# Second MLP in five sets of token tiles instead of four, and a first-MLP unit whose second token half begins a 512-byte line

## The chip, the cores and the metric

The kernel runs on one NeuronCore of a Trainium2 chip. Five engines work side by side, each with its own queue that it works off in order: TensorE (PE in the profile; its weight loads are shown apart as PEld), VectorE (DVE), ScalarE (ACT), GpSimd (POOL) and SyncE (SP, which here issues DMAs). The metric is the device time of one execution in microseconds (us), the median of several runs.

## The reference

Three blocks follow each other, all in float32 (the weights of both MLPs come as float64):

```
attn = softmax(mask(q k^T / 8)) v            # 4 batches, 8 heads, 576 tokens, head size 64
x    = attn as (4, 576, 512)

h    = relu(x @ w_in)                        # first MLP, 512 -> 1024
c    = conv over tokens, width 3, of h       # per channel
x    = (h * sigmoid(c)) @ w_out              # 1024 -> 512

u    = x + real(fft2(x))                     # over tokens and channels
un   = (u - mean) / sqrt(var + 1e-6)         # per token
out  = u + relu(un @ w_ch1) @ w_ch2          # second MLP, 512 -> 2048 -> 512
```

## The kernel before, in words

Matmuls run on float32 numbers rounded to fp32r. Each operand is split into a high and a low part, and a product takes three matmuls (`mm3`: high by high, high by low, low by high).

No instruction is issued where the code makes it. Every call records a piece of work with its reads, its writes, a due time (`key`) and a guessed duration for each engine that may do it. At the end `P.order()` (line 292) walks through a simulated time, gives each engine the ready piece of work with the earliest due time, and so fixes the order of every engine's queue and, where several engines may do a copy, the engine. A change of the recorded work thus also moves its neighbours.

**First MLP.** The work is cut into units: batch `b` (576 tokens) and slice `f` (128 of the 1024 channels), 32 in all. `m1` (line 644) computes a unit's hidden slice, the convolution and the gate, and writes the gated slice in its high part `gh` and low part `gl` into the tile `hid`. Both are stored with the second half of the tokens in reverse order, so that the Fourier transform can fold the halves. `m2` (line 672) uses 128-token pieces of `gh` and `gl` as the stationary operand of matmuls with 512 output columns, into banks 4 to 7 of PSUM. The pieces start at the columns in `COLS`; the 32 tokens left over of each half are copied into the tiles `g9`, which are multiplied once per two batches (`shared_tile`). 2304 tokens so make 18 tiles of 128: 16 regular ones and two shared ones, which stand at places 8 and 17 of the list `order`.

**Transform.** `dft(b, ...)` does the Fourier transform of a batch from small tables (tile `tb`) and writes u. For the batches 0 and 1 it also normalises the tiles (`ln`: statistics and a Newton square root on DVE, scaling on ACT, four transposes on PE, a split into high and low parts). Batch 0 goes straight into `first4`, batch 1 over DRAM (`to_dram`). The later tiles are normalised during the second MLP (`ln_set`).

**Second MLP.** The tiles are processed in sets (`SETS`, line 947). For a set and a slice `f` of 128 of the 2048 channels, `n1` (line 981) multiplies weights with the set's normalised tiles: up to 512 tokens are one matmul wide, a set of five tiles is done as two halves of 320. ACT makes the high part of the hidden slice, DVE the low part. `n2` (line 1003) multiplies 128-token pieces of it with the second weights, one PSUM bank per tile, over all `f`. `runs` (line 949) lists which set runs over which `f` with which banks; set 0 runs in two parts. The first eight slices' weights have homes in space that the first MLP leaves free; the last eight are converted from float64 (`W2.convert`, four DVE instructions and a copy each, through two buffers `raw`) while the second run is under way, since their space is the transform's.

`h_bank` hands out the PSUM banks 2 and 3 in turn for `n1`, so an `n1` can't begin before the low part of the one before the last has been read out of its bank by DVE.

Of the kernel before, what the change touches and what calls it, by code (L numbers as in the profile page):

```python
# [11 lines left out]
F32 = mybir.dt.float32  # L12
F32R = mybir.dt.float32r
# [9 lines left out]
B, H, S, D = 4, 8, 576, 64  # L23
DM, FF1, FF2 = 512, 1024, 2048
NF1, NF2 = FF1 // 128, FF2 // 128
HS = S // 2
# [165 lines left out]
class Plan:  # L192
# [79 lines left out]
    def mm3(self, o, ah, al, bh, bl, first, last):  # L272
        self.mm(o, ah, bh, first, False)
        self.mm(o, ah, bl, False, False)
        self.mm(o, al, bh, False, last)
# [142 lines left out]
def tile_kernel(ctx: ExitStack, tc: tile.TileContext, forms, qt_in, ktp, ktd, vtp, vtd, wm1, wm2, conv_w,  # L418
                tab, mask, ident16_in, ident_in, out):
    nc = tc.nc  # L420
    ctx.enter_context(tc.manual_schedule())
    P = Plan({"ACT": nc.scalar, "DVE": nc.vector, "POOL": nc.gpsimd, "PE": nc.tensor, "SP": nc.sync})
    mm, mm3, dma = P.mm, P.mm3, P.dma
# [11 lines left out]
    def copy(out_, in_, engines=("ACT",), key=None):  # L435
        n = out_.n()
        psum = in_.tile.pool is banks
        t = {"ACT": on_act(n), "DVE": on_dve(n, False, psum), "POOL": on_pool(n)}
        P.run({e: t[e] for e in engines}, "copy", key, out=out_, in_=in_)
# [4 lines left out]
    def lo_of(out_, src, hi, key=None):  # L444
        n, psum = out_.n(), src.tile.pool is banks
        dve("tensor_tensor", on_dve(n, True, psum), key, out=out_, in0=src, in1=hi.bitcast(F32), op=ALU.subtract)
# [11 lines left out]
    bank = [banks.tile([128, 512], F32, f"pb{i}", whole=True) for i in range(8)]  # L458
# [20 lines left out]
    win = stg.tile([128, 512], I32, "win")  # L479
    moe = pool_of("moe", reuse_waits="tile")  # L480
    x_odd = moe.tile([128, 4, 2, S], F32R, "x")
    hid_t = moe.tile([128, 2, 2, 640], F32R, "hid")
    cv_t = moe.tile([128, S], F32, "cv")
    g_t = moe.tile([128, S], F32, "g")
    hpad = [moe.tile([128, S + 2], F32, "hp") for _ in range(2)]
    moe.fill(-moe.size)
    gh_t, gl_t = ([hid_t[:, i, l, :S] for i in range(2)] for l in range(2))

    low = pool_of("low", reuse_waits="tile")
    g9h, g9l = (low.tile([128, NF1, 128], F32R, "g9") for _ in range(2))  # L490
# [147 lines left out]
        dve("tensor_tensor", 0.1, out=convw, in0=a, in1=r, op=ALU.add)  # L638


    COLS = [0, 128, 288, 416]
    hid = {}

    def m1(b, f, h_banks, at):
        s = NF1 * b + f
        w = W1.tiles[0, f]
        hp = hpad[s % 2]
        for half in range(2):
            o = of("h", h_banks)[:, :HS]
            sl = slice(HS * half, HS * half + HS)  # L650
            with P.products(at + 4.3 * half):
                for c in range(4):
                    wsl = slice(128 * c, 128 * c + 128)
                    mm3(o, w[:, 0, wsl], w[:, 1, wsl], xT[b][:, c, 0, sl], xT[b][:, c, 1, sl], c == 0, c == 3)
            P.run({"ACT": 0.41}, "activation", out=hp[:, 1 + HS * half:1 + HS * half + HS], in_=o, func=AF.Relu,
                  scale=0.5)
        cv, g = cv_t, g_t
        P.run({"ACT": 0.78}, "mul", out=cv, in_=hp[:, 1:S + 1], mul=convw[:, NF1 + f:NF1 + f + 1])
        dve("scalar_tensor_tensor", 0.81, out=cv, in0=hp[:, 0:S], scalar=convw[:, f:f + 1], in1=cv,
            op0=ALU.mult, op1=ALU.add)  # L660
        dve("scalar_tensor_tensor", 0.88, out=cv, in0=hp[:, 2:S + 2],
            scalar=convw[:, 2 * NF1 + f:2 * NF1 + f + 1], in1=cv, op0=ALU.mult, op1=ALU.add)
        P.run({"ACT": 0.69}, "activation", out=cv, in_=cv, func=AF.Tanh)
        dve("scalar_tensor_tensor", 0.54, out=g[:, 0:289], in0=cv[:, 0:289], scalar=1.0, in1=hp[:, 1:290],
            op0=ALU.add, op1=ALU.mult)
        dve("scalar_tensor_tensor", 0.48, out=g[:, 289:576], in0=cv[:, 575:288:-1], scalar=1.0,
            in1=hp[:, 576:289:-1], op0=ALU.add, op1=ALU.mult)
        gh, gl = hid[s] = gh_t[s % 2], gl_t[s % 2]
        copy(gh, g, ("ACT", "POOL"))
        lo_of(gl, g, gh)  # L670

    def m2(b, f, at):
        gh, gl = hid[NF1 * b + f]
        w = W1.tiles[1, f]
        for i in range(4):
            c0 = COLS[i]
            with P.products(at + 2.15 * i):
                mm3(bank[4 + i], gh[:, c0:c0 + 128], gl[:, c0:c0 + 128], w[:, 0], w[:, 1], f == 0, f == NF1 - 1)
        for src, dst in ((gh, g9h), (gl, g9l)):
            sv = src.bitcast(F32).rearrange("p (t s) -> p t s", t=2)[:, :, 256:288]  # L680
            dv = dst[:, f, :].rearrange("p (t s) -> p t s", t=2)[:, :, 32 * (b % 2):32 * (b % 2) + 32]
            P.run({"ACT": 0.235, "POOL": 0.45}, "copy", out=dv, in_=sv)

# [98 lines left out]
    def ln(us, puts, bank_of, at):  # L782


        n = len(us)
        mv = D_["mv"]()[:, :n]
        sq = D_["sq"]()
        v, r, t = (sq[:, i, :n] for i in range(3))
        for i in range(n):
            st = D_["st"]()  # L790
            dve("bn_stats", 0.68, out=st, in_=us[i])
            dve("bn_aggr", 0.17, out=mv[:, i], in_=st)
        small = lambda op_, **kw: dve(op_, 0.16, **kw)
        small("tensor_scalar", out=v, in0=mv[:, :, 1], scalar1=1e-6, scalar2=None, op0=ALU.add)

        small("tensor_scalar", out=r.bitcast(I32), in0=v.bitcast(I32), scalar1=-0.5,
              scalar2=float(0x5F3759DF), op0=ALU.mult, op1=ALU.add)
        small("tensor_scalar", out=v, in0=v, scalar1=-0.5, scalar2=None, op0=ALU.mult)
        for _ in range(3):
            small("tensor_tensor", out=t, in0=r, in1=r, op=ALU.mult)  # L800
            small("tensor_tensor", out=t, in0=t, in1=v, op=ALU.mult)
            small("scalar_tensor_tensor", out=r, in0=t, scalar=1.5, in1=r, op0=ALU.add, op1=ALU.mult)
        small("scalar_tensor_tensor", out=t, in0=mv[:, :, 0], scalar=-1.0, in1=r, op0=ALU.mult, op1=ALU.mult)
        for i in range(n):
            P.run({"ACT": 0.62}, "activation", out=us[i], in_=us[i], func=AF.Identity, scale=r[:, i:i + 1],
                  bias=t[:, i:i + 1])
            bt = bank_of()
            with P.products(at):
                for c in range(4):
                    P.turn(bt[:, 128 * c:128 * c + 128], us[i][:, 128 * c:128 * c + 128], ident)  # L810
            hi, lo, done = puts[i]()
            b4 = bt.rearrange("p (c n) -> p c n", c=4)
            copy(hi, b4)
            lo_of(lo, b4, hi)
            done()

    def to_dram(i):

        ns = D_["ns"]()
        return ns[:, 0], ns[:, 1], lambda: dma(n_dram[i], ns.rearrange("p l c n -> p l (c n)").bitcast(F32))  # L820
# [21 lines left out]
    def dft(b, at, every):  # L842
# [4 lines left out]
        when = [at - every]  # L847
# [52 lines left out]
        for m, T in enumerate((AT, BT)):  # L900
            for l in range(2):
                src = T[:, l, :, 256:288].bitcast(F32)
# [34 lines left out]
        if bp:  # L937
            y9 = yload(16 + pr)
            finish(16 + pr, y9, *products(lambda l, c: t9[0][:, l, c], lambda l, c: t9[1][:, l, c], a09))
            if b == 1:  # L940
                ln([y9], [lambda: to_dram(8)], df, when[0] + 8)
        pair(0)

    SETS = (range(0, 4), range(4, 9), range(9, 14), range(14, 18))
    R0 = 8
    runs = ((0, 0, R0, (4, 5, 6, 7)), (1, 0, 16, (0, 1, 4, 5, 6)), (0, R0, 16, (7, 0, 1, 4)),
            (2, 0, 16, (5, 6, 7, 0, 1)), (3, 0, 16, (4, 5, 6, 7)))  # L950
    hidden, rings, sets = {}, {}, []

    def un_load(p):
        for i, k in enumerate(SETS[p]):
            dma(sets[0][:, :, :, 128 * i:128 * i + 128].bitcast(F32),
# [100 lines left out]
    for k in range(2 * NF1):  # L1056
        _, i, f = W1.todo[k]
# [61 lines left out]
    for r, f in seq:  # L1119
        if r == 0:  # L1120
            begin[r, f] = T4 + 14 + 7.5 * f, 7.5
        else:
            step = 1.38 * len(SETS[runs[r][0]])
            begin[r, f] = at, step
            at += step
    lns = ({(2, 9 + i): (2, (i,)) for i in range(5)})
    lns.update({(3, 3 + i): (3, (i,)) for i in range(4)})
    for k, (r, f) in enumerate(seq):
        if (r, f) == (1, 0):
            later = pool_of("set", "left", (low,), reuse_waits="tile")  # L1130
            sets.append(later.tile([128, 2, 4, 640], F32R, "unt"))
            un_load(1)
        if (r, f) == (1, 2):
            wpb = pool_of("wpb", "right", (D_["pool"], keep), reuse_waits="tile")
            rest = [wpb.tile([128, 2, 512], F32R, "wf") for _ in range(2 * NF1)]
            ln_tiles_of(wpb)
            rings["u"].views += [wpb.tile([128, DM], F32, "uu") for _ in range(3)]
            rings["o"].views += [wpb.tile([128, DM], F32, "oo") for _ in range(2)]
            wpb.fill(TOP - wpb.size)
            for j in range(2 * NF1):  # L1140
                W2.convert(rest[j], raws[j % 2])
        at, step = begin[r, f]
        if (r, f) in lns:
            p, ids = lns[r, f]
            ln_set(p, ids, at + step * 0.9)
        n1(runs[r][0], f, at, step)
        n2(r, f, at + step, step)
# [80 lines left out]
```

## Time and profile before

| | us |
|---|---|
| runs | 775.37, 776.19, 777.86 (median 776.19) |
| profiled execution | 778.47 |
| its span, first to last instruction | 776.7 |
| PE busy | 744.8 (96%) |
| DVE busy | 486.7 (63%) |
| ACT busy | 308.6 (40%) |
| POOL busy | 135.9 (17%) |

The profiled execution is 2.28 us above the median of the runs; 1.8 us of it lie outside the span. PE is busy through nearly all of the span. Busy time alone says little where matmuls overlap: the distance from the start of one group of matmuls to the start of the next is what a group costs. The granted clock of TensorE is 1.00 where it runs at 2.4 GHz and 0.50 at 1.2 GHz.

The stretches of the span: attention of the first batch until about 60 us, attention beside the first MLP until about 250, first MLP beside the transforms until about 345, transforms beside the first part of set 0 until about 412, and the rest of the second MLP until 773.

### The profile page before, as it was taken

The numbers are of one execution on the slowest core, as the hardware profiler recorded it, in microseconds if no ns is written. First come the engines' busy times: TensorE is split into PE (matmuls) and PEld (weight loads), VectorE is DVE, ScalarE is ACT, GpSimd is POOL, SyncE is SP. The second block draws the span as 40 slices with busy tenths as digits, with TensorE's granted clock in tenths as the row PEclk, the third lists the DMA queues.
The fourth block names the chain that finished last, engine by engine and source line by source line (L and its number), as shares of the span: only waits on it lengthen the run. The fifth ranks groups of instructions, "written<-read, shape, count | busy, mean of one in ns | idle before, by whom it ended". The sixth has DMA issues, their size and how long they took to land.

```text
span 776.7 us, 11954 instructions
## 1 busy us (share of the span) xinstructions
PE 744.8 (96%) x4438; PEld 663.2 (85%) x4438; DVE 486.7 (63%) x1155; ACT 308.6 (40%) x792; POOL 135.9 (17%) x151
## 2 busy tenths in 40 slices
PE   5889989999999999989999999999999999999997
PEld 4779879998999998867788999988889999988886
DVE  5989989889888788979677667317544111121112
ACT  3877766675667655434332122112212111101110
POOL 4654424542445112201000000000000000000000
PEclk9979999999999999989999999999999999999999
DMA  9944354223412835357947333005131000030001
GB/s 239 254 152 134 107 164 139 88 72 111 152 48 90 285 120 163 107 190 250 330 162 246 136 133 135 1 1 163 42 105 32 28 1 1 1 122 1 1 0 55
DMA packets 38976, 88.58 MB, mean 114 GB/s; under 512 B 4351, under 2 KB 9859, under 8 KB 38790
## 3 DMA queue, kind: packets, MB, share of 16 engines
q1 hardware_dynamic: 38262, 84.66, 34.1%
q0 software_dynamic: 432, 2.97, 1.0%
q8 instruction: 35, 0.57, 0.3%
q10 hardware_dynamic: 224, 0.18, 0.1%
q14 instruction: 23, 0.19, 0.1%
HBM read 65.23 MB, written 22.44 MB: 113 GB/s over the span
## 4 chain that ended last, share of the span: by engine, by line
PE 53%; DVE 1%; ACT 0%; issue 0%; ACTq 0%
PE pb L259 53%; DVE y L246 0%; DVE hid L246 0%; DVE win L246 0%; DVE pm L246 0%; DVE raw L246 0%; DVE hp L246 0%; DVE pp L246 0%; ACT pq L246 0%; ACT pm L246 0%; ACTq L246 0%
## 5 line engine op out<-in xcount | busy, mean ns | idle before, releaser
L259 PE MATMUL pb<-wf,hid 128*128 128x512 f32 x1140 | 291.5, 397 | 1.2 <-DVE hid L246 1.2
L259 PEld LDWEIGHTS pb<-wf,hid 128*128 128x128 f32 x1140 | 207.6, 189 | 39.1 <-DVE hid L246 1.6
L246 DVE SCALAR_TENSOR_TENSOR hid<-pb,hid 128x320 fp32r<-128x320 f32 (+1 forms) x96 | 53.5, 557 | 186.5 <-ACT hid L246 186.4
L246 ACT ACTIVATE hid<-pb 128x320 fp32r<-128x320 f32 (+1 forms) x96 | 47.1, 491 | 256.7 <-PE pb L259 256.7
L259 PE MATMUL pb<-x,wf 128*128 128x288 f32 x768 | 116.6, 302 | 3.3 <-DVE wf L246 2.0
L259 PEld LDWEIGHTS pb<-x,wf 128*128 128x128 f32 x768 | 108.8, 191 | 7.0 <-DVE wf L246 2.2
L259 PE MATMUL pb<-unt,wf 128*128 128x320 f32 x672 | 103.6, 309 | 0.0
L259 PEld LDWEIGHTS pb<-unt,wf 128*128 128x128 f32 x672 | 100.8, 188 | 2.3
L246 POOL PARTITION_ALL_REDUCE mx<-sm x56 | 82.9, 1486 | 80.6 <-DVE sm L246 39.5
L259 PE MATMUL pb<-wf,wf 128*128 128x512 f32 x336 | 85.1, 400 | 3.6 <-DVE hid L246 3.6
L259 PEld LDWEIGHTS pb<-wf,wf 128*128 128x128 f32 x336 | 64.0, 193 | 17.5 <-DVE hid L246 4.3
L605 ACT ACTIVATE xb<-pb,rs 72x64 f32<-72x64 f32 (+1 forms) x224 | 51.2, 309 | 13.2 <-DVE rs L246 12.9
L246 DVE SCALAR_TENSOR_TENSOR cv<-hp,convw,cv 128x576 f32<-128x576 f32 x64 | 55.4, 866 | 1.3 <-ACT cv L246 0.7
L259 PEld LDWEIGHTS pb<-VT,sm 104*72 104x72 f32 (+1 forms) x448 | 41.0, 157 | 8.6 <-ACT sm L246 6.8
L259 PE MATMUL pb<-VT,sm 104*72 104x65 f32 (+1 forms) x448 | 42.8, 240 | 5.6 <-ACT sm L246 5.6
L259 PE MATMUL pb<-QT,KT 128*104 128x144 f32 (+1 forms) x224 | 44.3, 323 | 1.6 <-ACT sm L246 1.1
L259 PEld LDWEIGHTS pb<-QT,KT 128*104 128x104 f32 (+1 forms) x224 | 36.1, 191 | 7.5 <-issue 4.9
L246 ACT ACTIVATE hp<-pb 128x288 f32<-128x288 f32 x64 | 26.6, 416 | 29.9 <-PE pb L259 28.5
L246 DVE TENSOR_TENSOR wf<-raw,wf 128x512 fp32r<-128x512 f32 x44 | 31.7, 722 | 6.9 <-ACT wf L246 6.6
L246 DVE SCALAR_TENSOR_TENSOR raw<-raw,win 128x512 uint32<-128x512 uint32 x48 | 34.9, 727 | 0.9
L246 DVE SCALAR_TENSOR_TENSOR win<-raw,win 128x512 int32<-128x512 int32 x48 | 34.7, 723 | 1.0
L246 POOL CAST g<-hid 128x64 fp32r<-128x64 f32 x43 | 22.4, 528 | 73.4 <-ACT hid L246 37.1
(143 smaller groups left out, 842.6 us busy)
## 6 DMA issues: line engine op xcount, KB each, us to landing
raw<-in_wm_dram SPq DMA_DIRECT2D x48, 512.0 KB, 4.5
y<-yd SPq DMA_DIRECT2D x18, 256.0 KB, 4.2
ud<-y SPq DMA_DIRECT2D x18, 256.0 KB, 3.5
QT<-in_qt_dram SPq DMA_DIRECT2D x31, 144.0 KB, 3.4
fd<-fs SPq DMA_DIRECT2D x8, 514.0 KB, 3.9
fl<-fd SPq DMA_DIRECT2D x8, 514.0 KB, 6.3
yd<-y SPq DMA_DIRECT2D x16, 256.0 KB, 2.2
uu<-ud SPq DMA_DIRECT2D x16, 256.0 KB, 3.1
```

Source lines behind the costliest of these rows:

```text
L246: getattr(self.engines[eng], name)(**a)
L259: getattr(self.engines["PE"], name)(*[v.real() for v in a], **kw)
L605: nc.scalar.mul(out=x[:, i], in_=p[:, i], mul=r[:, i:i + 1])
```

## The change

- The sets become 4, 4, 4, 4 and 2 tiles instead of 4, 5, 5 and 4. All but the last then run `n1` as one 512-wide matmul per weight piece, the last as one 256-wide.
- The shared tile at place 8 now begins set 2 instead of ending set 1. Its normalisation inside `dft(1, ...)` goes; `ln_set` makes it later.
- The half-unit layout in `hid`: the second token half begins at column 384 (1536 bytes) instead of 288 (1152 bytes), and the pieces start at 0, 128, 384 and 512. The tile grows from 640 to 768 columns. The writes of `gh` and `gl` become two stretches of 288 instead of one of 576.
- `unt`, the tile of normalised tokens, shrinks from 640 to 512 columns; the scratch of GpSimd's DMAs from 2048 to 1024 bytes.

```diff
-    hid_t = moe.tile([128, 2, 2, 640], F32R, "hid")
+    hid_t = moe.tile([128, 2, 2, 768], F32R, "hid")
...
-    gh_t, gl_t = ([hid_t[:, i, l, :S] for i in range(2)] for l in range(2))
+    gh_t, gl_t = ([hid_t[:, i, l].rearrange("p (t s) -> p t s", t=2)[:, :, :HS] for i in range(2)] for l in range(2))
...
-    COLS = [0, 128, 288, 416]
+    COLS = [(0, 0), (0, 128), (1, 0), (1, 128)]
...
-        copy(gh, g, ("ACT", "POOL"))
-        lo_of(gl, g, gh)
+        gs = g.rearrange("p (t s) -> p t s", t=2)
+        copy(gh, gs, ("ACT", "POOL"))
+        lo_of(gl, gs, gh)
...
-                mm3(bank[4 + i], gh[:, c0:c0 + 128], gl[:, c0:c0 + 128], w[:, 0], w[:, 1], f == 0, f == NF1 - 1)
+                mm3(bank[4 + i], gh[:, t, c0:c0 + 128], gl[:, t, c0:c0 + 128], w[:, 0], w[:, 1], f == 0, f == NF1 - 1)
...
-            if b == 1:
-                ln([y9], [lambda: to_dram(8)], df, when[0] + 8)
...
-    SETS = (range(0, 4), range(4, 9), range(9, 14), range(14, 18))
+    SETS = (range(0, 4), range(4, 8), range(8, 12), range(12, 16), range(16, 18))
     R0 = 8
-    runs = ((0, 0, R0, (4, 5, 6, 7)), (1, 0, 16, (0, 1, 4, 5, 6)), (0, R0, 16, (7, 0, 1, 4)),
-            (2, 0, 16, (5, 6, 7, 0, 1)), (3, 0, 16, (4, 5, 6, 7)))
+    runs = ((0, 0, R0, (4, 5, 6, 7)), (1, 0, 16, (0, 1, 4, 5)), (0, R0, 16, (6, 7, 0, 1)),
+            (2, 0, 16, (4, 5, 6, 7)), (3, 0, 16, (0, 1, 4, 5)), (4, 0, 16, (6, 7)))
...
-    lns = ({(2, 9 + i): (2, (i,)) for i in range(5)})
+    lns = {(2, 9 + i): (2, (i,)) for i in range(4)}
     lns.update({(3, 3 + i): (3, (i,)) for i in range(4)})
+    lns.update({(4, 5 + i): (4, (i,)) for i in range(2)})
...
-            sets.append(later.tile([128, 2, 4, 640], F32R, "unt"))
+            sets.append(later.tile([128, 2, 4, 512], F32R, "unt"))
...
-    nc = _bacc.Bacc("TRN2", target_bir_lowering=False, num_devices=1, dynamic_dma_scratch_size=2048)
+    nc = _bacc.Bacc("TRN2", target_bir_lowering=False, num_devices=1, dynamic_dma_scratch_size=1024)
```

What stands in the queues, first on PE in the second run (`pb_128` and `pb_129` are the PSUM banks 2 and 3, `pb_126`, `127`, `130`, `131`, `132` the banks 0, 1, 4, 5 and 6; `unt` the set's tokens, `hid` the hidden slice). Before, one slice `f` is:

```order
L259 MATMUL pb_129<-unt,wf 128x320 x12
L259 MATMUL pb_128<-unt,wf 128x320 x12
L259 MATMUL pb_126<-wf,hid 128x512 x3
L259 MATMUL pb_127<-wf,hid 128x512 x3
L259 MATMUL pb_130<-wf,hid 128x512 x3
L259 MATMUL pb_131<-wf,hid 128x512 x3
L259 MATMUL pb_132<-wf,hid 128x512 x3
```

After, two slices of the second run are:

```order
L259 MATMUL pb_129<-unt,wf 128x512 x12
L259 MATMUL pb_126<-wf,hid 128x512 x3
L259 MATMUL pb_127<-wf,hid 128x512 x3
L259 MATMUL pb_130<-wf,hid 128x512 x3
L259 MATMUL pb_131<-wf,hid 128x512 x3
L259 MATMUL pb_128<-unt,wf 128x512 x12
```

Per slice there are 39 matmuls before and 24 after, for five tiles and for four. The last run of the changed kernel has, per slice, twelve matmuls of 256 columns and six of 512.

The second place is on DVE, at the end of the first MLP. `hid<-pb_129` reads the result of set 0's first `n1` out of bank 3; `y` are tiles of u, `st`, `mv` and `sq` the statistics of `ln`. Before:

```order
L246 TENSOR_TENSOR pp<-pq,pm 128x258
L246 TENSOR_TENSOR pm<-pq,pm 128x258
L246 TENSOR_TENSOR y<-y,pp 128x255
L246 TENSOR_TENSOR y<-y,pm 128x257
L246 BN_STATS st<-y 128x6
L246 BN_AGGR mv<-st 128x2
...
L246 SCALAR_TENSOR_TENSOR sq<-mv,sq 128x1
L246 SCALAR_TENSOR_TENSOR g<-cv,hp 128x287
L246 SCALAR_TENSOR_TENSOR hid<-pb_129,hid 128x512
```

After:

```order
L246 TENSOR_TENSOR hid<-g,hid 128x2x288
L246 SCALAR_TENSOR_TENSOR hid<-pb_129,hid 128x512
L246 SCALAR_TENSOR_TENSOR win<-raw,win 128x512
L246 SCALAR_TENSOR_TENSOR raw<-raw,win 128x512
L246 COPY y<-pb_130 128x512
L246 TENSOR_TENSOR pp<-pq,pm 128x258
L246 TENSOR_TENSOR pm<-pq,pm 128x258
L246 TENSOR_TENSOR y<-y,pm 128x257
L246 TENSOR_TENSOR y<-y,pp 128x255
```

The shared tile's statistics are gone from here, and the read of bank 3 has moved ahead of the four instructions that finish that tile. Further on in the same queue, the changed kernel has the copy of the second shared tile out of bank 2 (`o<-pb_128`), which ACT did before, behind the statistics of batch 1's first two tiles:

```order
L246 SCALAR_TENSOR_TENSOR sq<-mv,sq 128x2
L246 TENSOR_TENSOR o<-y 128x255 x2
L246 TENSOR_TENSOR fo<-fo,o 128x255 x2
L246 TENSOR_TENSOR fo<-y 128x2
L246 COPY o<-pb_128 128x512
L246 TENSOR_TENSOR e_187<-o 64x512
```

PE's next use of bank 2 stands behind that copy.

## Rows read from the trace of the kernel before

**Rows 1.** Windows: stretch, then us of busy time (instructions) per engine, granted clock

```profile
266.00:412.00 146.00, 138.95 (x823) 121.21 (x822) 122.14 (x309) 65.82 (x148) 20.34 (x36) 0.98 0.57 188
...
340.00:345.00 5.00, 4.90 (x12) 3.84 (x13) 3.63 (x7) 1.78 (x4) 1.41 (x2) 0.50 0.36 105
...
412.00:776.00 364.00, 360.64 (x1876) 316.71 (x1874) 132.72 (x327) 64.59 (x122) 0.85 (x1) 1.00 0.18 61
```

**Rows 2.** Chain of work that ended last, in order: start, us, what

```profile
384.95 387.70 PE pb L259 x2033
```

**Rows 3.** PE timeline, a set of five: start, us, engine, line, what

```profile
640.39 3.68 PE L259 MATMUL pb<-unt,wf 128*128 128x320 f32 x24
643.91 3.59 PE L259 MATMUL pb<-wf,hid 128*128 128x512 f32 x15
647.34 3.68 PE L259 MATMUL pb<-unt,wf 128*128 128x320 f32 x24
```

**Rows 4.** PE timeline, a set of four

```profile
701.75 2.88 PE L259 MATMUL pb<-wf,hid 128*128 128x512 f32 x12
704.48 2.88 PE L259 MATMUL pb<-wf,x 128*128 128x512 f32 x12
707.20 2.88 PE L259 MATMUL pb<-x,hid 128*128 128x512 f32 x12
```

**Rows 5.** PE timeline, 300 to 340 us, narrower matmuls

```profile
302.01 3.34 PE L259 MATMUL pb<-x,wf 128*128 128x288 f32 x24
305.19 1.03 PE L259 MATMUL pb<-ident,y 128*128 128x128 f32 x8
...
317.72 0.88 PE L259 MATMUL pb<-tb,BT 128*128 128x258 f32 x6
318.44 0.88 PE L259 MATMUL pb<-tb,AT 128*128 128x258 f32 x6
...
328.39 1.03 PE L259 MATMUL pb<-ident,y 128*128 128x128 f32 x8
329.18 1.63 PE L259 MATMUL pb<-wf,wf 128*128 128x512 f32 x6
```

**Rows 6.** PE timeline inside one unit of the first MLP's `m2`

```profile
284.63 1.78 PE L259 MATMUL pb<-wf,hid 128*128 128x512 f32 x7
```

```profile
286.02 1.79 PE L259 MATMUL pb<-wf,hid 128*128 128x512 f32 x7
```

**Rows 7.** PE timeline, 330 to 390 us, with idle time and releaser

```profile
340.10 5.43 PE L259 MATMUL pb<-wf,wf 128*128 128x512 f32 x12 [3.61 <-DVE hid L246]
...
358.73 1.20 PE L259 MATMUL pb<-wf,hid 128*128 128x512 f32 x4 [1.17 <-DVE hid L246]
...
384.95 1.20 PE L259 MATMUL pb<-x,hid 128*128 128x512 f32 x4 [1.31 <-DVE hid L246]
```

**Rows 8.** DVE timeline, 335 to 340 us

```profile
335.78 0.69 DVE L246 BATCH_NORM_STATS2 st<-y 128x6 f32<-128x512 f32 x1
...
339.36 0.68 DVE L246 SCALAR_TENSOR_TENSOR hid<-pb,hid 128x512 fp32r<-128x512 f32 x1
```

**Rows 9.** DVE timeline, 350 to 358 us

```profile
350.77 0.42 DVE L246 TENSOR_TENSOR pp<-pq,pm 128x258 f32<-128x258 f32 x1
...
357.20 0.16 DVE L246 TENSOR_TENSOR fo<-y 128x2 f32<-128x2 f32 x1
```

**Rows 10.** Second run: PE's first matmuls, and a weight's conversion ending on DVE

```profile
412.59 1.92 PE L259 MATMUL pb<-unt,wf 128*128 128x320 f32 x12
```

```profile
486.35 0.69 DVE L246 TENSOR_TENSOR wf<-raw,wf 128x512 fp32r<-128x512 f32 x1 [0.28 <-ACT wf L246]
```

**Rows 11.** DVE timeline, 701 to 712 us, a set of four

```profile
702.59 0.69 DVE L246 SCALAR_TENSOR_TENSOR hid<-pb,hid 128x512 fp32r<-128x512 f32 x1 [4.75 <-ACT hid L246]
```

**Rows 12.** The tile `tb`: its DMA's issues and their landing

```profile
L288 POOL DMA_DIRECT2D tb<-in_tab_dram x3: 555/562/691, 250.3 to 251.5; - x3
...
DMA to landing us min/median/max: 8.1/10.3/14.6
```

More of the change, by code (lines that the diff above doesn't have):

```diff
@@ L675, in m2 @@
         for i in range(4):
-            c0 = COLS[i]
+            t, c0 = COLS[i]
             with P.products(at + 2.15 * i):
-                mm3(bank[4 + i], gh[:, c0:c0 + 128], gl[:, c0:c0 + 128], w[:, 0], w[:, 1], f == 0, f == NF1 - 1)
+                mm3(bank[4 + i], gh[:, t, c0:c0 + 128], gl[:, t, c0:c0 + 128], w[:, 0], w[:, 1], f == 0, f == NF1 - 1)
         for src, dst in ((gh, g9h), (gl, g9l)):
-            sv = src.bitcast(F32).rearrange("p (t s) -> p t s", t=2)[:, :, 256:288]
+            sv = src.bitcast(F32)[:, :, 256:288]
             dv = dst[:, f, :].rearrange("p (t s) -> p t s", t=2)[:, :, 32 * (b % 2):32 * (b % 2) + 32]
```

## The prediction

> **What bounds the kernel now.** I read the chain of waits first: it ends in 387.70 us of matmuls on PE that begin at 384.95 [rows 2], so from there to the end PE waits for nobody and a microsecond of matmul work is a microsecond of time. Then the windows [rows 1]: from 412 to 776 the granted clock is 1.00, the upper of the two levels; from 266 to 412 PE is busy for 138.95 of 146.00, so 7.05 us are idle. Three waits with DVE as the releaser make 3.61 + 1.17 + 1.31 = 6.09 of these [rows 7]; 0.96 is left in smaller ones. The largest has a second price: right behind it twelve matmuls take 5.43 us [rows 7] where twelve of the same form take 2.88 elsewhere [rows 4], and the window 340 to 345 shows the clock at 0.50, the lower level [rows 1]. That is 2.55 more. The stretch before 412 so holds 7.05 + 2.55 = 9.6 us that PE loses, and the stretch after it nothing but the matmuls' own price. These are the two places where this change can pay. The timelines of PE and DVE then gave the prices.
>
> **Part A, the widths of `n1`.** Today a set of five costs, per slice, from one `n1` to the next, 647.34 - 640.39 = 6.95 us: 24 matmuls of 320 columns in 3.52 (146.7 ns each) and 15 of 512 in 3.43 [rows 3]. A set of four costs 707.20 - 701.75 = 5.45: 24 of 512 columns, at 2.73 / 12 = 227 ns [rows 4]. Before there are 32 slices of five and 32 of four; after, 64 of four and 16 of two. So 32 x 6.95 = 222.4 is replaced by 32 x 5.45 + 16 times the slice of two. That slice has six matmuls of 512 (6 x 0.227 = 1.36) and twelve of 256 columns, a width that this trace does not have. The nearest row is 258 columns: (318.44 - 317.72) / 6 = 120 ns [rows 5], hence 12 x 0.12 = 1.44 and 2.80 for the slice. New total 174.4 + 44.8 = 219.2, and A = **-3.2 us**. The columns are the same in sum; what goes is 192 matmuls. Bounds from the neighbours on both sides: 128 columns cost (329.18 - 328.39) / 8 = 99 ns and 288 columns (305.19 - 302.01) / 24 = 132.5 ns [rows 5]. With 192 such matmuls that is -4.0 or +2.4, so A lies between -7.2 and -0.8.
>
> What a matmul costs over its columns at 2.4 GHz is in these rows a fixed 13 ns or so: 227 - 213 at 512, 147 - 133 at 320, 132.5 - 120 at 288, 120 - 107.5 at 258. The Trainium skill, "TensorE: Matmul & The Clock Gate", section "Wait — 56ns, not 53.3ns?", has a much smaller fixed cost, about 2.5 ns for a matmul at the upper clock. By that figure leaving out 192 matmuls would give only 0.5 us (an estimate from that page); the trace does not agree, its rows show five times as much at four widths.
>
> **Part B, the unit layout.** The second token half's pieces, which PE loads as stationary operands, come to begin at a multiple of 512 bytes. In the unit's `m2` the first group of seven matmuls, six of them with an aligned piece, takes 1.78 us, the second, six of them with an unaligned one, 1.79 [rows 6]; by its columns' starts 0 and 128 the one, 288 and 416 the other. A matmul there is about 4 ns above the 227 of [rows 4]. No difference by position is seen, so **0**. If all of the excess went, 384 such matmuls would give 384 x 4 ns = -1.6. The writes of `gh` and `gl` in two stretches of 288: the one-stretch low part takes about 0.7 like any 512-wide one (0.68 in [rows 8]); 32 of them at a tenth more would be 2 us of DVE time beside PE-bound work, and I put them at 0 with +0.5 as the upper end. The smaller DMA scratch concerns POOL's three loads of `tb`, issued at 250.3 to 251.5 and landing within 8.1 to 14.6 us [rows 12], and the tables are first used at 266.6; the third could be late by some microseconds unseen, since the first matmuls need the first part only: 0, with +1.
>
> **Part C, the shared tile's `ln` leaves the transform.** Before the 3.61 us wait DVE works through that `ln`, from 335.78 to 339.36 [rows 8], 3.6 us with one gate operation of 0.4 in it, and only then reads bank 3, which PE's next `n1` needs. In the new order the read of bank 3 stands ahead even of the tile's last four operations. The 3.61 wait and the 2.55 of lower clock behind it go: -6.16.
>
> What is late next: the copy of the second shared tile out of bank 2 (`o<-pb_128`), which goes from ACT to DVE. Queued ahead of it on DVE, from the moment PE ends the batch's last `m2`: the copy of `y` 0.69 (as in [rows 11]), four operations on halves 4 x 0.42, the next pair of tiles with its `ln` 357.20 - 350.77 = 6.43 [rows 9], about six half-wide folds at 0.4, and the copy itself 0.69: 11.9 us. PE has meanwhile, by its queue, 21 `m2` matmuls at 0.231 [rows 6], 13 of 258 columns at 0.12 [rows 5], 18 of 512 at 0.227 [rows 4] and 0.4 of transposes: 4.85 + 1.56 + 4.09 + 0.4 = 10.9. So PE would wait some 1.0 to 1.2 there, in place of the 1.17 at 358.73 [rows 7]. Behind PE's waiting matmul stand the transform's next products; the engines that wait for these (ACT's copies, DVE's folds) have their own queues to work off. At 384.95 the old order had the three steps of a weight's conversion ahead of the read; the new order has the read first, so 1.31 goes too. I keep 1.2 (new) + 0.96 (small ones) + 1.0 (unforeseen, in a queue that is reshuffled for 140 us) = 3.2 of the 9.6: C = **-6.4 us**, within -9.6 (no wait left) and 0 (all of it comes back elsewhere).
>
> The tile's `ln` itself is done later, within the second MLP, where DVE is busy for 132.72 of 364.00 us [rows 1]: it costs nothing as long as no weight is late. The second run's weights are converted on DVE up to 486.35 + 0.69 = 487.0, 74.5 us after the run's first matmul at 412.59 [rows 10]. Slices of 5.45 instead of 6.95 need the last weight 15 x 5.45 = 81.8 after the run's start, before 104.3. The cover shrinks from 30 us to 7, and to 4 with 3.2 us of `ln` among the conversions, but it is not gone. In the last run, with 2.8 us a slice, the path from the end of `n1` to the low part's end on DVE is 703.28 - 701.75 = 1.53 us [rows 4, 11], and `n2` of the slice before and the next `n1` lie between: hidden.
>
> **Sum.** -3.2 + 0 - 6.4 = -9.6, on the profiled execution's 778.47: 768.9. That execution is 2.28 above the median of the runs, so **766.6 us** where 776.19 stands.
>
> **Rivals.** (1) *The waits only move.* For it: 140 us of reshuffled queues in which DVE is busy for 122 of 146 us [rows 1], so each `ln` or fold is a possible new wait. Against: the change takes 3.2 us of DVE work out of just this stretch. Then A alone is left: 776.19 - 3.2 = 773.0 (769 to 775.4 by A's bounds). (2) *The excess per matmul is in the columns, not the count.* Then A is 0 and C stays: 776.19 - 6.4 = 769.8. Against it stand four widths with the same excess.
>
> Beside rival 2: the fixed cost of the Trainium skill's page "TensorE: Matmul & The Clock Gate", cited above, comes within 0.5 us of its time; the trace, with 13 ns, does not agree.
>
> (3) *Aligned pieces do load faster*, and the change does in B what two equal rows deny: -1.6, 765.0. (4) *Slower: the second run overtakes its weights.* The place is the second run, where PE would wait for `wf` from DVE. It decides from the point where the conversions need 81.8 - 3.2 = 78.6 us instead of 74.5, 6% more. If they are a fifth slower, because each waits for DMA and ACT (the last shows 0.28 of waiting for ACT [rows 10]) and now has a low part of 512 columns every 5.45 us among them, that is 89.4 + 3.2 - 81.8 = 10.8 us of waiting, and 2.55 more as the clock falls behind a long wait: 766.6 + 13.4 = 780.0.
>
> **How the numbers follow.** What a measurement of this kernel can tell from no change is about 0.3%, 2.3 us. Forecast 0.65 (its own range 763 to 771: C between -9.2 and -3, A between -4 and -2.2); rival 1 0.17, most of it below 773.9, a third within the 0.3%; rival 2 0.06; rival 3 0.06; rival 4 0.06, its milder half around no change. Faster so 0.65 + 0.11 + 0.06 + 0.06 = 0.88, less a little for the forecast's own tail: 0.87; same 0.08; slower 0.05. The range for 8 in 10 takes the forecast's, and most of rival 1: 763 to 773.5.
>
> **What would show it.** A: all slices of 5.45 us from start to start, the last run's of 2.80 with 256-column matmuls at about 120 ns; right if the second MLP after 412 is shorter by 3 us. B: the groups of seven `m2` matmuls still at 1.78. C: no wait of 3.6 us on DVE's read of bank 3, the window where it stood at clock 1.00, and instead a wait of about 1 us on the copy `o`; idle from 266 to the second run's start down from 7 to about 3 us. The forecast is wrong if that idle time is still above 6 us, if a second clock drop appears, or if PE waits for `wf` in the second run.

## The result and the profile after

The changed kernel takes 766.33 us (765.86 to 766.87), the kernel before 776.46 beside it; the ratio is 0.9874 with an interval of 0.9858 to 0.9889. Run again with the experiments below it took 766.92 against 776.3 (0.9878, 0.9862 to 0.9894). These ratios are estimates over the runs; the quotient of the two medians can differ from them by up to 0.001, as it does here (0.9869). The prediction was 766.6.

The windows of the changed kernel, with the columns of [rows 1]:

```profile
266.00:412.00 146.00, 143.45 (x846) 125.07 (x845) 126.19 (x306) 66.18 (x150) 17.81 (x35) 1.00 0.59 194
340.00:345.00 5.00, 5.00 (x24) 4.14 (x23) 4.57 (x21) 0.14 (x1) 0.00 (x0) 1.00 0.66 230
412.00:776.00 364.00, 349.06 (x1648) 292.20 (x1646) 125.65 (x309) 60.88 (x104) 1.33 (x2) 1.00 0.17 56
```

PE's idle time from 266 to 412 falls from 7.05 us to 146.00 - 143.45 = 2.55, and the window that stood at 0.50 is at 1.00. PE's timeline has four waits left in this stretch (idle time and releaser in brackets):

```profile
303.39 1.36 PE L259 MATMUL pb<-ident,y 128*128 128x128 f32 x8 [0.23 <-ACT y L246]
305.39 1.20 PE L259 MATMUL pb<-wf,hid 128*128 128x512 f32 x4 [0.17 <-DVE hid L246]
...
346.87 0.65 PE L259 MATMUL pb<-ident,y 128*128 128x128 f32 x4 [1.39 <-ACT y L246]
...
354.16 1.07 PE L259 MATMUL pb<-tb,fl 128*128 128x290 f32 x6 [0.65 <-DVE a L246]
```

All three waits of [rows 7] are gone; the largest is now 1.39 us, and no slow matmuls follow it. From 354.16 the chain of waits is PE alone (this answers to [rows 2]):

```profile
354.16 406.91 PE pb L259 x1967
```

The second MLP's slices, from the start of one `n1` to the next. In a set of four (compare [rows 4]):

```profile
641.35 2.88 PE L259 MATMUL pb<-wf,wf 128*128 128x512 f32 x12
644.07 2.88 PE L259 MATMUL pb<-wf,hid 128*128 128x512 f32 x12
646.79 2.88 PE L259 MATMUL pb<-wf,x 128*128 128x512 f32 x12
```

and in the set of two:

```profile
722.88 1.60 PE L259 MATMUL pb<-unt,wf 128*128 128x256 f32 x12
724.32 1.55 PE L259 MATMUL pb<-wf,hid 128*128 128x512 f32 x6
725.70 1.60 PE L259 MATMUL pb<-unt,x 128*128 128x256 f32 x12
```

646.79 - 641.35 = 5.44 and 725.70 - 722.88 = 2.82; twelve matmuls of 256 columns take 1.44, 120 ns each.

The gain by place, in the two profiled executions: the second run's first matmul is at 412.59 in [rows 10] and, in the changed kernel, here:

```profile
403.50 1.75 PE L259 MATMUL pb<-unt,wf 128*128 128x512 f32 x7
```

From it to the chain's end are 772.65 - 412.59 = 360.06 us before and 761.07 - 403.50 = 357.57 after: **2.5 us less**. The rest, 9.1 us, lies ahead of it. Of this about 2 us are the executions' own difference: up to 272 us TensorE does the same work in the same order in both kernels, and with 1600 matmuls behind it TensorE stands at 244.25 before and at 242.38 after. (The profiled executions of the runs below, which also do that work, stand there between 241.13 and 243.79, and both of these ends have the old layout.) So some 7.1 us were won between 272 us and the second run.

### The profile page after: what moved, and what is told of

The parts are those of the page before. It is cut to its first block, busy times and chain, and to the rows that moved or that the text cites. A ratio compares the mean times of both kernels' runs of the same rounds, so it can differ in the third digit from the quotient of the medians.

```text
span 765.0 us, 11525 instructions
## 1 busy us (share of the span) xinstructions
PE 739.3 (97%) x4246; PEld 643.4 (84%) x4246; DVE 485.3 (63%) x1137; ACT 305.9 (40%) x777; POOL 135.6 (18%) x152
## 4 chain that ended last, share of the span: by engine, by line
PE 88%; DVE 7%; DMA 2%; ACT 2%; issue 1%; SPq 0%; DVEq 0%
PE pb L259 88%; DMA raw<-in_wm_dram 1%; DVE win L246 1%; DVE sm L246 1%; ACT xb L606 1%; DMA maskt<-in_mask_dram 1%; DVE y L246 1%; DVE sq L246 1%; DVE cv L246 0%; DVE fo L246 0%; DVE raw L246 0%; DVE wf L246 0%; DVE x L246 0%; DVE st L246 0%; ACT sm L246 0%
## 5 line engine op out<-in xcount | busy, mean ns | idle before, releaser
L246 DVE SCALAR_TENSOR_TENSOR hid<-pb,hid 128x512 fp32r<-128x512 f32 (+1 forms) x80 | 51.0, 637 | 181.8 <-ACT hid L246 181.7
L246 ACT ACTIVATE hid<-pb 128x512 fp32r<-128x512 f32 (+1 forms) x80 | 44.4, 555 | 249.5 <-PE pb L259 242.1
L259 PE MATMUL pb<-unt,wf 128*128 128x512 f32 (+1 forms) x504 | 103.3, 354 | 0.0
L259 PEld LDWEIGHTS pb<-unt,wf 128*128 128x128 f32 x504 | 85.0, 189 | 14.2
L259 PE MATMUL pb<-wf,wf 128*128 128x512 f32 x336 | 82.3, 392 | 0.0
L259 PEld LDWEIGHTS pb<-wf,wf 128*128 128x128 f32 x336 | 62.3, 188 | 12.6
L246 DVE TENSOR_TENSOR sm<-sm,mx 104x288 f32<-104x288 f32 (+1 forms) x56 | 33.6, 600 | 0.8 <-POOL mx L246 0.6
```

Of the source, the lines that this page charges most:

```text
L246: getattr(self.engines[eng], name)(**a)
L259: getattr(self.engines["PE"], name)(*[v.real() for v in a], **kw)
```

## The experiments

C undone, B undone, `n1` in two halves and C alone shared one chip, on which the kernel before took 775.9; the other four kernels, the changed one run again among them, shared another (776.3).

**C undone.** The shared tile's `ln` goes back into the transform, and set 2 loads the result:

```diff
+            if b == 1:
+                ln([y9], [lambda: to_dram(8)], df, when[0] + 8)
...
-            ln_set(p, ids, at + step * 0.9)
+            if (p, ids) == (2, (0,)):
+                dma(sets[0][:, :, :, 0:128].bitcast(F32), n_dram[8].rearrange("p l (c n) -> p l c n", c=4))
+            else:
+                ln_set(p, ids, at + step * 0.9)
```

> The changed kernel with the shared tile's normalisation put back into the second batch's transform, so that A (the set widths) and B (the unit layout) stand alone. By the theory (the gain is A plus C) the 3.6 us wait on DVE's read of bank 3 and the clock at the lower level behind it come back: about 773.3 us, 7 over the changed kernel's 766.3 (the prediction's own size for C, 6.4, would give 772.7). By the rival that the reshuffled queues or the layout made the gain and not the normalisation's leaving: below 768.5.

Measured 772.67 us, ratio 0.9953 (0.9937 to 0.9969). The old wait and the lower clock behind it are back, on PE's timeline and in the window:

```profile
337.72 5.49 PE L259 MATMUL pb<-wf,wf 128*128 128x512 f32 x12 [3.59 <-DVE hid L246]
```

```profile
338.00:343.00 5.00, 5.00 (x12) 3.74 (x13) 3.26 (x6) 1.44 (x3) 1.42 (x2) 0.50 0.39 105
```

Twelve matmuls take 5.49 us, with the clock at its lower level. A (with B) alone is 775.9 - 772.67 = 3.2 us by the medians (2.4 to 4.9 by the ratio's interval), where 3.2 was predicted; C is worth 5.4 us on top of it, against 767.24 for the changed kernel with the old layout on the same chip (5.8 against 766.92 on the other), somewhat under the predicted 6.4.

**B undone.** The old unit layout and the old scratch in the changed kernel:

```diff
-    hid_t = moe.tile([128, 2, 2, 768], F32R, "hid")
+    hid_t = moe.tile([128, 2, 2, 640], F32R, "hid")
...
-    COLS = [(0, 0), (0, 128), (1, 0), (1, 128)]
+    COLS = [0, 128, 288, 416]
...
-    dynamic_dma_scratch_size=1024
+    dynamic_dma_scratch_size=2048
```

> The changed kernel with the old layout of a unit (second half at column 288, 640 columns, one-stretch writes) and the old scratch of 2048 bytes; sets as changed, TensorE's queue the same. By the theory B is nothing: 766.3, within 0.5 us, and twelve m2 matmuls take as long as in the changed kernel. By the rival that aligned stationary pieces load faster: 767.9 or more.

> The changed kernel itself, unaltered, beside the others on one chip: 766.3 as before. It is what the kernel with the old layout (767.24) and those of this group are compared with; by the theory that the layout gives nothing it should lie within 0.6 us of 767.24 where the chip is like that one.

Measured 767.24 (766.84 to 768.65) with the old layout, and 766.92 (766.00 to 767.87) for the changed kernel run again. The spreads overlap, and 0.3 us is far below what can be told apart. The waits on PE have the same places and sizes in both. The traces are finer than the times: between 150 and 240 us one matmul of `m2` follows the other after 232 ns (median) in both kernels, and from PE's 1600th matmul to the second run's first they take 161.45 us with the old layout and 161.12 with the new. Rival 3 is out: no sign of its 4 ns a matmul, or 1.6 us, from aligned pieces. A smaller effect than about 1 us isn't excluded.

**`n1` in two halves.** In the sets 1 to 3 each matmul of 512 columns becomes two of 256 in the same bank, each with a weight load of its own:

```diff
-            if n <= 512:
+            if p in (0, 4):
...
+                if half == 0:
+                    bk = h_bank()
+                cols, cc = slice(256 * half, 256 * half + 256), range(4)
+                o = bk[:, cols]
```

> The changed kernel with n1 of the sets 1, 2 and 3 made as two halves of 256 columns in the same bank: 48 slices x 24 = 1152 matmuls more, the columns the same. By the theory of a fixed 13 ns a matmul (227 or 228 ns at 512, 119.4 at 256 in the changed kernel's trace, so 2 x 119.4 - 228 = 11 ns more per pair): 1152 x 11 to 12 ns = 12.7 to 13.8 us, 779.0 to 780.1. By the rival, a fixed cost of 2.5 ns: 2.9 us, 769.2. If the excess hangs on the columns alone: 766.3.

The expectation counted wrongly: of the 24 matmuls in a slice of four only 12 are `n1`, so 48 x 12 = 576 are added, not 1152. With that, a fixed 11 to 12 ns gives 6.3 to 6.9 us and a fixed 2.5 ns gives 1.4. Measured 774.91 us (773.65 to 777.19), 8.0 over the changed kernel on the other chip and 7.7 over the one with the old layout on the same chip. A slice now:

```profile
641.48 3.04 PE L259 MATMUL pb<-wf,wf 128*128 128x256 f32 x24
644.35 2.91 PE L259 MATMUL pb<-wf,hid 128*128 128x512 f32 x12
647.10 3.04 PE L259 MATMUL pb<-wf,wf 128*128 128x256 f32 x24
```

5.62 us instead of 5.44: 24 x 256 columns take 2.87 where 12 x 512 took 2.72, and `n2` behind them 2.75 instead of 2.72. 48 x 0.18 = 8.6. So a matmul more at the same columns costs (2.87 - 2.72) / 12 = 12.5 ns, 15 with the longer `n2`; why `n2` gets longer stays open. The count decides, rival 2 is out. Every matmul here has a weight load beside it (1648 and 1646 in the window from 412 us), so what was counted are pairs of the two, and no run parts the matmul's share from the load's. The Trainium skill, "TensorE: Matmul & The Clock Gate", section "Wait — 56ns, not 53.3ns?", has about 2.5 ns as the fixed cost of a matmul behind another; for these pairs the run does not agree.

**C alone.** In the kernel before, the shared tile's `ln` is left out and done nowhere (set 1's fifth tile takes tile 7's tokens):

```diff
-            if b == 1:
-                ln([y9], [lambda: to_dram(8)], df, when[0] + 8)
...
-                n_dram[k].rearrange("p l (c n) -> p l c n", c=4))
+                n_dram[min(k, 7)].rearrange("p l (c n) -> p l c n", c=4))
```

> The kernel before with C alone: the shared tile's normalisation is left out of the second batch's transform and done nowhere (set 1's fifth tile takes tile 7's tokens), sets and layout as before. By the theory: C alone, 6.4 as predicted or 7.1 as the two traces show it, so 769.4 to 770.1, with the bank 3 read ahead of the shared tile's last operations and no clock drop. By the rival that the waits only move: 774 to 776.5.

This theory fell, as it stood: 774.95 us (771.29 to 777.55), ratio 0.9981 (0.9961 to 1.0002), which can't be told from no change. The 3.6 us wait is gone, and beside the changed kernel's four waits PE has two new ones, as rival 1 would have it:

```profile
376.25 0.50 PE L259 MATMUL pb<-x,hid 128*128 128x512 f32 x1 [1.18 <-ACT x L246]
378.07 0.73 PE L259 MATMUL pb<-x,hid 128*128 128x512 f32 x2 [1.32 <-DVE x L246]
```

`x` is here the home of a second-MLP weight that comes late. DVE's queue shows why:

```profile
368.89 0.69 DVE L246 SCALAR_TENSOR_TENSOR hid<-pb,hid 128x512 fp32r<-128x512 f32 x1
373.02 0.69 DVE L246 SCALAR_TENSOR_TENSOR hid<-pb,hid 128x512 fp32r<-128x512 f32 x1 [3.44 <-ACT hid L246]
373.63 0.42 DVE L246 TENSOR_SCALAR win<-raw 128x512 int32<-128x512 int32 x1
```

The weight's conversion (`win<-raw`) stands behind a read of `n1`'s result, which DVE reaches 3.44 us too early. In the changed kernel the conversion comes first:

```profile
369.52 0.68 DVE L246 SCALAR_TENSOR_TENSOR hid<-pb,hid 128x512 fp32r<-128x512 f32 x1
370.14 0.43 DVE L246 TENSOR_SCALAR win<-raw 128x512 int32<-128x512 int32 x1
...
374.79 0.68 DVE L246 SCALAR_TENSOR_TENSOR hid<-pb,hid 128x512 fp32r<-128x512 f32 x1
```

The difference on SP ahead of it: a set 1 of five tiles needs five loads of `unt`, one of four needs four, and the weights' loads (`raw`) stand behind them. With the fifth, so the new theory, the planner takes the weight to arrive later and puts the read first. Two runs tested that.

**C alone with four loads.** As the last, but set 1's fifth tile is filled by GpSimd:

```diff
-        for i, k in enumerate(SETS[p]):
+        for i, k in list(enumerate(SETS[p]))[:4]:
...
+        for l in range(2):
+            P.run({"POOL": 1.0}, "copy", out=sets[0][:, l, :, 512:640], in_=sets[0][:, l, :, 384:512].bitcast(F32))
```

> The kernel before without the shared tile's normalisation (as in the run that had C alone, 774.95), and with set 1's fifth tile filled by a copy on GpSimd from its fourth in place of a DMA, so that SP issues four loads of unt there and not five. New theory: with five loads the queue of DVE has the read of bank 3, which waits 3.4 us for TensorE, ahead of the first weight's conversion, the weight for run 0 comes late, and TensorE waits 1.2 + 1.3 us and more in other runs; with four the conversion stands first again. Then C alone is worth its 6.4 to 7.1 us: 768.8 to 769.5. Rival, the fifth load has nothing to do with it: 774 to 775.5 again.

Measured 769.22 us (768.38 to 770.74), ratio 0.9910 (0.9892 to 0.9928): C's 7.1 us are there. They lie where they should: from the 1600th matmul to the second run's first PE takes 168.34 us in the kernel before, 161.45 here and 161.12 in the changed kernel, and from there to its last matmul 360.05, 359.96 and 357.57. The `ln` and the fifth load are both gone here; a kernel before with four loads and its `ln` was not run. The conversion is ahead again, and the two waits on `x` are gone:

```profile
369.67 0.43 DVE L246 TENSOR_SCALAR win<-raw 128x512 int32<-128x512 int32 x1 [0.38 <-DMA raw<-in_wm_dram]
...
373.98 0.68 DVE L246 SCALAR_TENSOR_TENSOR hid<-pb,hid 128x512 fp32r<-128x512 f32 x1
```

**A fifth load in the changed kernel** (with the old layout, which leaves the room):

```diff
-            sets.append(later.tile([128, 2, 4, 512], F32R, "unt"))
+            sets.append(later.tile([128, 2, 4, 640], F32R, "unt"))
             un_load(1)
+            dma(sets[0][:, :, :, 512:640].bitcast(F32), n_dram[7].rearrange("p l (c n) -> p l c n", c=4))
```

> The changed kernel with the old layout (767.24) and a fifth load that nothing needs, tile 7 once more into the columns 512 to 639 of a wider unt, ahead of the run that reads it. By the new theory the read of bank 3 moves ahead of the weight's conversion on DVE and TensorE waits for the weight x from 374 on, as in the run with C alone: 2.5 us by that trace, up to 6 by that kernel's median, so 769.7 to 773. By the rival: 767.2.

Measured 771.26 us (769.83 to 772.15), 4.0 over 767.24 and 4.3 over 766.92 on the same chip. The order on DVE has turned, and PE has the same waits at the same place:

```profile
376.74 0.50 PE L259 MATMUL pb<-x,hid 128*128 128x512 f32 x1 [1.18 <-ACT x L246]
378.56 0.73 PE L259 MATMUL pb<-x,hid 128*128 128x512 f32 x2 [1.32 <-DVE x L246]
```

```profile
373.51 0.69 DVE L246 SCALAR_TENSOR_TENSOR hid<-pb,hid 128x512 fp32r<-128x512 f32 x1 [3.44 <-ACT hid L246]
374.12 0.42 DVE L246 TENSOR_SCALAR win<-raw 128x512 int32<-128x512 int32 x1
```

So one load that nothing needs costs 4.0 us here and 5.7 in the kernel with C alone (774.95 - 769.22, on two chips), by way of the queue order. The rows show 2.5 us of it, and in both profiled executions the way from the 1600th matmul to the second run's first is 3.1 us longer (164.5 for 161.45). Where the rest goes in the other executions, which spread over 771.3 to 777.6 with C alone, stays open. Their mean granted clock was 0.991 in the profiled one (772.19) and 0.982 in the longest, so stretches at the lower level may be part of it; no long one was profiled.

**The copy `o` on ACT.** The wait that is left, 1.39 us:

```diff
-        copy(yl, a9, ("ACT", "DVE"))
+        copy(yl, a9, ("ACT",) if p else ("ACT", "DVE"))
```

> The changed kernel with the copy of the second shared tile out of bank 2 bound to ACT, as it was before; TensorE's order is the same. The 1.39 us that TensorE waits at 346.87 are released by ACT's scaling of y, which stands behind the evacuation of n1; the copy on DVE ended at 346.75, 0.5 before its user. If that copy is what sets the wait, it goes: about 765. If ACT's order sets it, as the trace's releaser says, nothing is gained: 766.3, or a little more since ACT now does the copy between the two scalings.

Measured 766.09 us (765.12 to 766.85), ratio to the kernel before 0.9867 (0.9851 to 0.9882): no difference from 766.92 that can be told. The wait stays what it was:

```profile
345.97 0.66 PE L259 MATMUL pb<-ident,y 128*128 128x128 f32 x4 [1.39 <-ACT y L246]
```

The copy on DVE was not what PE waited for. No version that clearly beats the changed kernel came out of these runs.

## Why the prediction was right

- **What bounds it.** PE's losses in 266 to 412 were 7.05 us idle and 2.55 us of lower clock. Undoing C brought the pair back, 3.59 us of wait and twelve matmuls in 5.49 us.
- **A, -3.2 us.** 3.2 by the run with C undone, 2.5 by the profiled executions' second MLP, which in the changed kernel also holds the four transposes of the moved tile (0.4 us). The price taken for 256 columns, 120 ns from 258-column rows, is what the trace shows; the slice of two takes 2.82 for 2.80. The fixed price per matmul held at a further size.
- **B, 0.** 767.24 us with the old layout, 766.92 with the new.
- **C, -6.4 us.** 7.1 us alone (with four loads), 5.4 to 5.8 on top of A. Of the 3.2 us of waiting expected to remain, 2.55 remained.
- **What is late next.** The time and about the size were right (1.0 to 1.2 us forecast, 1.39 measured); the instruction that waits and what it waits for were not. DVE took 346.75 - 335.11 = 11.64 us from the copy of `y` to the end of the copy `o`, for the 11.9 forecast. But PE reaches the transposes of `y` before its next use of bank 2, and these wait for ACT. DVE's timeline, then ACT's:

```profile
335.11 0.69 DVE L246 COPY y<-pb 128x512 f32<-128x512 f32 x1 [0.78 <-PE pb L259]
...
344.46 0.16 DVE L246 SCALAR_TENSOR_TENSOR sq<-mv,sq 128x2 f32<-128x2 f32 x1
...
346.06 0.69 DVE L246 COPY o<-pb 128x512 f32<-128x512 f32 x1
```

```profile
345.52 0.60 ACT L246 ACTIVATE hid<-pb 128x512 fp32r<-128x512 f32 x1 [5.38 <-PE pb L259]
346.01 1.51 ACT L246 ACTIVATE y<-y,sq 128x512 f32<-128x512 f32 x2
```

DVE's last statistics instruction, which the scaling `y<-y,sq` needs, is done at 344.62; ACT stands idle until 345.52 for an evacuation of `n1` that is ahead in its queue. The forecast followed DVE's queue and not ACT's.
- **The second run's weights** (rival 4). Rival 4 did not come: PE has no wait from the second run on. The forecast read the conversion at 486.35 as the last. It is the last but one, the last slice's weight for `n1`; that for `n2` follows and ends 489.55 + 0.69 - 412.59 = 77.7 us after the run's first matmul. In the changed kernel the two end 472.99 + 0.68 - 403.50 = 70.2 and 476.18 + 0.69 - 403.50 = 73.4 us after it, earlier and not later than before. PE needs the first of them 15 x 5.44 = 81.6 us after it, so the cover is 11 us where the forecast had 4. DVE before, then after:

```profile
489.55 0.69 DVE L246 TENSOR_TENSOR wf<-raw,wf 128x512 fp32r<-128x512 f32 x1 [0.71 <-ACT wf L246]
```

```profile
472.99 0.68 DVE L246 TENSOR_TENSOR wf<-raw,wf 128x512 fp32r<-128x512 f32 x1
...
476.18 0.69 DVE L246 TENSOR_TENSOR wf<-raw,wf 128x512 fp32r<-128x512 f32 x1 [0.71 <-ACT wf L246]
```

- **What it missed.** The step that C's wait simply goes was right only together with part of A that had no term: set 1 of four tiles has a load less on SP. With the five loads the order of DVE's queue turns and C alone is worth about 1 us by the medians (774.95 for 775.9), which can't be told from nothing. The forecast read the new order of the changed kernel, which has both, so the sum came out; as a statement on C by itself it would have been wrong, and rival 1, at 0.17, described just that.
- **How close.** That the sum came within 0.3 us of the median is partly luck. In the profiled executions the part ahead of the second run gave some 7.1 us for the 6.4 of C and the part behind it 2.5 for the 3.2 of A, so two misses of 0.7 cancel, and the changed kernel's own runs spread over 2 us (765.86 to 767.87).

## What to carry to other kernels

With an order that a planner makes, parts of a change needn't add up: try each part alone, and read all the queues of the kernel that will run, the waiter's as well as the releaser's. A wait of 3.6 us was priced rightly only with the lower clock behind it, 2.55 us more. Where TensorE is the bound and the columns are given, count the matmuls with their weight loads, and take the price of a new width from the nearest width in the trace.

## What the runs showed of the hardware

Matmuls of fp32r that each load weights of their own (128x128) cost 13 to 14 ns over their columns at 2.4 GHz at the three widths measured between 256 and 512 (120 ns at 256, 147 at 320, 227 at 512), and twelve of 512 columns behind twenty-four of 256 take 2.75 us instead of 2.72. Not expected was how far one transfer of 512 KB that nothing needs (128 partitions of 1024 float32) can reach: 4.0 and 5.7 us through the order of another engine's queue.
